# A two-layer attention and MLP kernel on Trainium2: the MLP's first product rewritten as seven smaller products

## The chip, the core and the metric

The kernel runs on one core of one Trainium2 chip. The core has five engines that run side by side, each through its own instructions in program order: TensorE (PE: matmuls, with weight loads shown apart as PEld), VectorE (DVE), ScalarE (ACT), GpSimd (POOL) and SyncE (SP), whose only work here is to issue DMA transfers. The metric is device time in microseconds (us), the median of three runs.

## The reference

Two rounds of the same pair of blocks, with the same weights, on x of 2048 rows by 640 (all float32):

```python
x = x + attention(layernorm(x), wqkv, wo)      # 32 heads of 20
x = x + mlp(layernorm(x), w1, b1, w2, b2)
# mlp: h = layernorm(x) @ w1 + b1   (640 -> 1536)
#      r = max(h, 0); h = r * r
#      out = h @ w2 + b2            (1536 -> 640)
```

## The kernel before, in words

One layer is: the projections to q, k and v; attention over 32 blocks; the output projection (`add_heads`); and the MLP in two stages, **up** (first product, with ReLU and square) and **down** (second product). The activations h go through DRAM between the two (`d_h`, `d_h1`).

Numbers are float32. For TensorE each operand is split in a high part and a rest (`split_to`: ScalarE copies, VectorE subtracts), and a product is the sum of three matmuls (`THREE`: high by high, high by rest, rest by high).

Up works on blocks of 512 rows (`qb` from 0 to 3). One of the 12 output tiles of 128 is a chain of 15 matmuls (`chain`, L376): 5 contraction tiles of 128 times the three of `THREE`, each with 128x128 weights and 512 moving columns, into one of the eight PSUM banks; the banks go round (`ps_all`). Two chains make a unit `j`; six units make a block. After a chain ScalarE applies ReLU with the bias (L1361); after a unit VectorE squares (L1369) and, for blocks whose second product is by Strassen, makes a sum and a difference (L1372, L1375).

The rows come to up normalised and transposed. For block 0 of a layer `normal_rows` normalises and TensorE turns 20 tiles (`transposed`, L1329). For blocks 1 to 3 `turned_rows` does it during the block ahead: per 128 rows, VectorE takes the statistics (L284, L285; GpSimd makes the inverse root), normalises into a tile y (L317) and transposes 32x32 squares (L322); SP writes that to DRAM (`d_t`) and reads it back turned, by four loads (`turn_load`); then `parts` splits it (L339, L340).

What an engine does beside a stage is handed out by `side()`: it takes one entry of the list `steps` at each call, so the list fixes where in each engine's own program order this side work stands. An engine that waits holds up everything behind it in its queue.

Down takes the 2048 rows in eight units of 256. Where Strassen is used, a unit has a first group of four products and a second of three (`grp` 0 and 1), each over three steps `j`; `make` prepares the operands two steps ahead, `fetch` reads h back. Weights stand split in SBUF slots of 128 x 1024 (42 slots for everything); `w_1` (120 pieces of 128, 15 slots) and `w_2` are prepared by GpSimd during the attention of layer 1 (`prep_job`), written to DRAM and loaded in every layer; 14 of the loads of `w_2` are asked for in block 0 of up, 14 in block 3.

## Time and profile before

| | |
|---|---|
| median of three runs | 3515.46 us (3514.46 to 3515.82) |
| the profiled execution: its time, its span | 3517.9 us, 3516.1 us |
| mean granted TensorE clock | 0.999 |
| busy: PE, DVE, ACT, POOL | 3504.1, 2732.5, 2733.7, 828.0 us |
| up, layer 2: its 720 matmuls | 3200.85 to 3364.08 us |
| down, layer 2 | 3364.08 us to the end |

The page gives busy time, not the use that is made of it. Matmuls are pipelined: their durations overlap, so the time a stage takes on TensorE is read from how far apart the matmuls start, not from their mean duration. In a row of the groups the last figures are the busy time in us, the mean ns of one instruction, and the idle time of the engine ahead of them with what ended it.

### The profile page before, as it was taken

The page shows a single profiled execution, that of the slowest core. Times are in us where ns is not written, and L with a number is a line of the kernel's source. Part 1 is how long each engine was busy: PE and PEld are TensorE (multiplying, and loading weights), DVE is VectorE, ACT ScalarE, POOL GpSimd, SP SyncE. Part 2 cuts the span into 40 slices and gives each one's busy share as a digit, 9 for nine tenths or more (in the row PEclk, how much of TensorE's full clock was granted, in tenths as well). Part 3 has the DMA queues.
Part 4 walks back from the last instruction along what each step waited for, and adds up shares of the span by engine and source line. Part 5 has one row for each costly group of instructions (what it writes and reads, how often), then busy time and mean ns, then how long its engine had stood idle before and what let it go on. Part 6 is the DMA issues. An engine that isn't in the chain of part 4 may idle for free.

```text
span 3516.1 us, 71077 instructions
## 1 busy us (share of the span) xinstructions
PE 3504.1 (100%) x25292; PEld 2112.9 (60%) x25292; DVE 2732.5 (78%) x5326; ACT 2733.7 (78%) x4804; POOL 828.0 (24%) x975
## 2 busy tenths in 40 slices
...
GB/s 259 234 207 188 143 170 134 135 126 133 60 55 60 42 103 192 310 198 237 234 195 224 194 180 69 77 76 57 77 76 55 53 58 50 103 196 308 195 253 141
DMA packets 325378, 514.87 MB, mean 146 GB/s; under 512 B 74532, under 2 KB 149796, under 8 KB 325024
## 3 DMA queue, kind: packets, MB, share of 16 engines
...
## 4 chain that ended last, share of the span: by engine, by line
PE 96%; DMA 2%; ACT 1%; POOL 0%; DVE 0%; issue 0%; SPq 0%; POOLq 0%; ACTq 0%; DVEq 0%
PE banks L810 28%; PE banks L795 18%; PE banks L701 18%; PE banks L376 13%; PE banks L1455 9%; PE banks L396 6%; PE banks L408 5%; PE banks L391 0%; PE banks L508 0%; ACT e L805 0%; DMA x<-d_x 0%; DMA x<-in_A_x_dram 0%; SPq L78 0%; DMA few<-d_s 0%; DMA o<-d_r 0%
## 5 line engine op out<-in xcount | busy, mean ns | idle before, releaser
L805 ACT ACTIVATE e<-banks 128x512 f32<-128x512 f32 (+1 forms) x3416 | 2035.1, 691 | 56.3 <-PE banks L795 21.5
L712 DVE TENSOR_REDUCE mx<-banks 128x1 f32<-128x512 f32 x2560 | 1620.3, 685 | 321.6 <-PE banks L701 274.4
L810 PE MATMUL banks<-e,vg 128*32 128x512 f32 x8192 | 1093.5, 605 | 2.2 <-ACT e L805 2.1
L701 PE MATMUL banks<-k,q 60*128 60x512 f32 x3360 | 1060.1, 411 | 0.9 <-DMA q<-d_qk 0.9
L795 PE MATMUL banks<-q,k 62*128 62x512 f32 x4096 | 1049.0, 441 | 1.2 <-ACT v L472 0.6
L795 PEld LDWEIGHTS banks<-q,k 62*128 62x128 f32 x4096 | 514.6, 184 | 748.5 <-ACT e L805 440.9
L701 PEld LDWEIGHTS banks<-k,q 60*128 60x128 f32 x3360 | 568.0, 185 | 196.4 <-ACT e L805 64.2
L741 DVE CUSTOM_DVE_ANT_0 rl<-banks,rl 128x512 f32<-128x512 f32 x736 | 477.0, 689 | 31.1 <-PE banks L701 6.7
L734 ACT ACTIVATE rl<-banks 128x512 f32<-128x512 f32 x736 | 399.7, 602 | 57.0 <-PE banks L701 46.5
L810 PEld LDWEIGHTS banks<-e,vg 128*32 128x32 f32 x8192 | 162.2, 108 | 353.5 <-issue 270.6
L408 PE MATMUL banks<-xnT,wqk 64*128 64x512 f32 x1080 | 327.7, 393 | 0.0
L376 PE MATMUL banks<-xnT,w 128*128 128x512 f32 x1440 | 327.0, 389 | 0.0
L396 PE MATMUL banks<-xnT,wqk 64*128 64x512 f32 x1080 | 326.9, 395 | 0.0
L376 PEld LDWEIGHTS banks<-xnT,w 128*128 128x128 f32 x1440 | 270.2, 188 | 56.0
L1361 ACT ACTIVATE r<-banks,b_t 128x512 f32<-128x512 f32 x96 | 66.2, 690 | 222.1 <-PE banks L376 205.1
L854 POOL TENSOR_TENSOR few<-few,minus_t 128x16 f32<-128x16 f32 x62 | 179.9, 2902 | 239.4 <-DMA few<-d_s 234.4
L701 PE MATMUL banks<-kd,q 60*128 60x512 f32 x736 | 210.1, 398 | 0.8 <-ACT rl L734 0.6
L408 PEld LDWEIGHTS banks<-xnT,wqk 64*128 64x128 f32 x1080 | 202.1, 188 | 8.5
L396 PEld LDWEIGHTS banks<-xnT,wqk 64*128 64x128 f32 x1080 | 200.3, 187 | 11.1 <-issue 1.7
L865 POOL TENSOR_TENSOR o<-o 128x512 f32<-128x512 f32 x62 | 79.6, 1284 | 508.6 <-DMA o<-d_r 285.5
L308 POOL CAST mr<-nt 128x32 fp32r<-128x32 f32 x64 | 13.5, 212 | 775.9 <-DVE nt L767 775.9
L396 PE MATMUL banks<-wv,xnT 64*128 64x320 f32 x960 | 193.5, 308 | 0.0
...
## 6 DMA issues: line engine op xcount, KB each, us to landing
q<-d_qk SPq DMA_DIRECT2D x876, 80.0 KB
...
k<-d_qk SPq DMA_DIRECT2D x444, 80.0 KB
...
d_o<-ot SPq DMA_DIRECT2D x248, 80.0 KB
```

What stands on the lines that cost most here:

```text
L376: nc.tensor.matmul(dst, a, b, start=(n == 0), stop=(n == last))
L396: top = nc.tensor.matmul(dst, a[:64], b[:64], start=start, stop=last)
L408: low = nc.tensor.matmul(dst, a, b, start=False, stop=last, skip_group_check=True)
L701: nc.tensor.matmul(dst, q_t[t][b : b + 60, p, sub * P : (sub + 1) * P], k_t[t // NQB, c][b : b + 60, p, :], start=True, stop=True,)
L712: nc.vector.tensor_reduce(maxima(t)[:, 2 * p + par, sub, c : c + 1], dst, axis=AX.X, op=ALU.max)
L734: nc.scalar.activation(r, dst, AF.Relu)
L741: nc.vector.tensor_tensor_reduce(out=r[par], in0=dst, in1=r[par], scale=1.0, scalar=LEAST, op0=ALU.add, op1=ALU.max, accum_out=maxima(t)[: ...
L795: nc.tensor.matmul(dst, k_t[t // NQB, kt // 4][b : b + 62, p, (kt % 4) * P : (kt % 4 + 1) * P], q_t[t][b : b + 62, p, :], start=True, stop ...
L805: nc.scalar.activation(dst, src, AF.Exp, scale=SCALE)
L810: nc.tensor.matmul(acc[32 * h : 32 * h + 32, :], v_t[t // NQB, kt // 8][:, kt % 8, 32 * h : 32 * h + 32], es[p][:, par, :], start=(kt == 0 ...
L854: nc.gpsimd.tensor_tensor(few, few, minus_t, op=ALU.pow)
L1455: nc.tensor.matmul(dst, a, b, start=first and not more, stop=last, skip_group_check=more)
```

## The change

The contraction of 640 is cut into two halves of two tiles (4 of 5 tiles) and the fifth tile. On the four tiles a unit `j`, which has 2 halves of its output (tiles j and j + 6) and 2 halves of the 512 rows, is computed by Strassen's seven products (in Winograd's form) of 128 x 256 by 256 x 256; the fifth tile is added into four of them (`extra`). A product is 6 or 9 matmuls of 256 moving columns (L1427 in the changed kernel). A unit has 54 of them, in place of 30 of 512 columns. The products stand in four banks of a half of PSUM, and three of the seven are added on top of one that VectorE has already read: S3 on S2's bank, A12 on A11's, S4 on S1's. VectorE now adds products (five additions of 256 columns a unit), ScalarE does ReLU and all squares, GpSimd makes the sum and the difference for down. S4 of a unit is issued after A11 of the next (`tail`, `finish`).

The rows of all blocks, block 0 too, are turned by VectorE and DRAM (`forms`), and for each pair of 128-row tiles GpSimd makes sums and differences, ScalarE copies the high parts and VectorE or GpSimd subtracts. `forms` has 33 or 31 yields, spread over the 42 `side()` calls of a block; for block 0 they stand in the last two blocks of `add_heads`. TensorE's transposes of up are gone.

`w_1` is prepared by `put_first` in sums and differences: 192 pieces, 24 slots; 16 are loaded in `add_heads`, 8 in block 0 of up. All 28 slots of `w_2` that down needs at first are loaded in block 3 of up (15) and in down (13), and down's first two units go side by side, so that each weight piece serves two units in a row. The matmuls of down are the same in kind and number.

TensorE, the start of up in layer 1, before (xnT: the transposed rows; w: weights) and in the changed kernel, one unit (xf, xd: the operands made by `forms`):

```order
L1329 MATMUL banks<-ident,x_16301 128x128
L376 MATMUL banks<-xnT_16461,w_15975 128x512 x3
L376 MATMUL banks<-xnT_16468,w_15975 128x512 x3
L376 MATMUL banks<-xnT_16475,w_15975 128x512 x3
L376 MATMUL banks<-xnT_16482,w_15975 128x512 x2
L376 MATMUL banks<-xnT_16482,w_15977 128x512
```

```order
L1427 MATMUL banks<-xf_16414,w_16237 128x256 x6
L1427 MATMUL banks<-xf_16420,w_16095 128x256 x6
L1427 MATMUL banks<-xf_16421,w_16095 128x256 x3
L1427 MATMUL banks<-xf_16415,w_16237 128x256 x6
L1427 MATMUL banks<-xf_16416,w_16239 128x256 x6
L1427 MATMUL banks<-xf_16417,w_16239 128x256 x6
L1427 MATMUL banks<-xd_16422,w_16243 128x256 x3
L1427 MATMUL banks<-xf_16418,w_16241 128x256 x6
```

The chain into one bank has become runs of six; the second and third row are S4 of the unit ahead.

VectorE, in the second half of block 0 of up in layer 1, before:

```order
L1369 TENSOR_TENSOR r_16757<-r_16757 128x1024
L1372 TENSOR_TENSOR s_16803<-r_16757 128x256
L1375 TENSOR_TENSOR r_16757<-r_16757 128x2x128
L340 TENSOR_TENSOR xnT_16743<-y_16653,xnT_16743 128x128
L340 TENSOR_TENSOR xnT_16745<-y_16653,xnT_16745 128x128
```

and in the changed kernel, from the tail of its second unit through its third (units counted 0 to 5: units 1 and 2; us holds u0 and u1, t is GpSimd's sums):

```order
L353 STREAM_TRANSPOSE x_16733<-y_16866 128x640
L1488 TENSOR_TENSOR r_16826<-banks,us_16749 128x2x128
L1465 TENSOR_TENSOR us_16858<-banks,us_16858 128x256
L376 TENSOR_TENSOR xf_16904<-y_16745,xf_16904 128x2x128
L376 TENSOR_TENSOR xf_16905<-t_16903,xf_16905 128x2x128
L1473 TENSOR_TENSOR us_16858<-banks,us_16858 128x256
L1474 TENSOR_TENSOR r_16941<-banks,us_16858 128x2x128
L1475 TENSOR_TENSOR r_16941<-banks,us_16858 128x2x128
```

The rests of two operands of the next block (L376: B11 and T2) now stand between the additions that read the unit's own banks (L1465 reads S2, L1473 S3, L1474 S1, L1475 A22, L1488 S4).

SP, the transfers of block 0 (d_t: the transposed tiles in DRAM; y_16773: the turned tile 2, which T2 needs), in the changed kernel:

```order
L78 DMA y_16745<-d_t 32x4x160 x4
L78 DMA d_t<-x_16731 128x640
L78 DMA d_h<-r_16723 128x1024
L78 DMA d_h_111<-us_16662 128x256
L78 DMA w_16852<-d_w_99 128x1024
L78 DMA y_16773<-d_t 32x4x160 x4
L78 DMA d_t<-x_16733 128x640
```

The load of tile 2 stands behind the write of tile 1 and two stores of unit 0.

The diff, cut to its core:

```diff
@@ -201,12 +201,16 @@
-    w_1 = Split("w1", P, NF * 2 * KD)
+    w_1 = Split("w1", P, NP * 32)
     w_2 = Split("w2", HALF, NP * 16)
-    def at_1(f, hw):
-        return ((f % NP) * 2 + f // NP) * 2 * KD + hw * KD
+    LAST = 7
+    A11, S2, S1, A22, S3, A12, S4 = range(LAST)
+    B11, T2_, T1_, T4_, T3_, B21, B22 = range(LAST)
+    def at_1(j, p, hw=0, k=0):
+        return j * 32 + p * 4 + hw * 2 + k
...
+    def put_first(j, a, b):
+        t = xtile("t")
+        k1, k2, k3 = slice(0, 2 * P), slice(2 * P, 4 * P), slice(4 * P, D)
+        def put(p, part):
+            w_1.put(part, at_1(j, p), at_1(j, p, 1), 2, pool_hi, pool_lo)
+        nc.gpsimd.tensor_tensor(t[:, k1], b[:, k1], b[:, k2], op=ALU.add)
+        pool_lo(t[:, k2], t[:, k1], a[:, k1])
+        pool_lo(b[:, k1], a[:, k1], b[:, k1])
+        put(A11, a[:, k1])
+        yield
...
-    def parts(res, i, y):
...
-    def turned_rows(qb, x_src, ys):
...
+    def forms(qb, x_src, res, late):
+        xs, ys, mvs = {}, {}, {}
+        def view(y):
+            return y.rearrange("p (a k i) -> p k a i", a=4, k=KD)
+        def split(dst, src, i, lo):
+            hi_, lo_ = (
+                dst[:, h, :, i * P : (i + 1) * P].rearrange("p k (a i) -> p k a i", a=4)
+                for h in range(2)
             )
+            nc.scalar.copy(hi_, src)
+            lo(lo_, src, hi_.bitcast(F32))
+        def pair(i):
+            a, b = view(ys[i]), view(ys.pop(i + 2))
+            t = xtile("t").rearrange("p (k a i) -> p k a i", a=4, k=KD)
+            k1, k2, k3 = slice(0, 2), slice(2, 4), slice(4, 5)
...
+            dve = nc.vector.tensor_sub
+            pool_lo(t[:, k1], b[:, k1], a[:, k1])
+            pool_lo(t[:, k2], b[:, k2], t[:, k1])
+            split(res[B11], a[:, k1], i, dve)
+            yield
+            pool_lo(b[:, k1], b[:, k2], b[:, k1])
+            split(res[T2_], t[:, k2], i, dve)
+            yield
+            split(res[T1_], t[:, k1], i, dve)
+            yield
+            pool_lo(t[:, k3], a[:, k3], b[:, k3])
+            pool_lo(t[:, k2], a[:, k2], t[:, k2])
+            split(res[B22], b[:, k2], i, dve)
+            yield
+            split(res[T4_], t[:, k2], i, pool_lo)
+            yield
+            split(res[T3_], b[:, k1], i, pool_lo)
+            yield
+            for r, y in enumerate((a, b)):
+                split(res[LAST][:, :, r : r + 1], y[:, k3], i, dve)
+            split(res[LAST + 1], t[:, k3], i, dve)
+            yield
+            if not late:
+                split(res[B21], a[:, k2], i, dve)
+                del ys[i]
+                yield
+        def rest():
+            res[B21] = slot([P, 2, 2, 2 * P], F32R, "xf")
+            for i in range(2):
+                split(res[B21], view(ys.pop(i))[:, 2:4], i, nc.vector.tensor_sub)
+        def load(i):
+            xs[i] = row_tile(x_src, qb * 4 + i)
+        def turned(i):
+            ys[i] = turn(xs[i], mvs.pop(i), i)
+            del xs[i]
+        load(0)
+        load(2)
+        yield
+        yield
+        yield
+        for i in (0, 2):
+            mvs[i] = stats(xs[i])
+            yield
+        load(1)
+        load(3)
+        yield
+        for i in (0, 2):
+            turned(i)
+            yield
+            yield
+        for i in (1, 3):
+            mvs[i] = stats(xs[i])
+            yield
+        turn_load(ys[0], 0)
+        turned(1)
+        yield
+        turn_load(ys[2], 2)
+        yield
+        turned(3)
+        yield
+        yield
+        yield
+        turn_load(ys[1], 1)
+        for n, _ in enumerate(pair(0)):
+            if n == 1:
+                turn_load(ys[3], 3)
+            yield
+        yield from pair(1)
+        if late:
+            late.append(rest)
...
-    def normal_rows(qb, x_src, res):
...
-    def transposed(xs):
...
-    def up(qb, xnt, whole, side):
...
+    class Up:
+        def __init__(self, side):
+            self.side, self.n, self.tail, self.held = side, 0, None, []
+        def chain(self, dst, j, p, x, more, extra=None):
+            todo = [
+                (w_1.piece(at_1(j, p, hw, k)), x[p][:, hx, k, :])
+                for k in range(2)
+                for hw, hx in THREE
+            ]
+            if extra is not None:
+                i, rows = extra
+                todo += [(w_1.piece(at_1(j, LAST, i) + hw), rows[:, hx, :]) for hw, hx in THREE]
+            for n, (w, v) in enumerate(todo):
+                nc.tensor.matmul(
+                    dst, w, v, start=n == 0 and not more, stop=n == len(todo) - 1,
+                    skip_group_check=more,
                 )
+        def dst(self, b):
+            return banks[:, 4 * (self.n % 2) + b, : 2 * P]
+        def finish(self):
+            if self.tail:
+                self.tail()
+                self.tail = None
+        def store(self):
+            while self.held:
+                self.held.pop(0)()
+        def flush(self):
+            self.finish()
+            self.store()
+        def unit(self, qb, j, x, whole, free):
+            side = self.side
+            us = xtile("us")
+            u0, u1 = us[:, : 2 * P], us[:, 2 * P : 4 * P]
+            last, diff = x[LAST], x[LAST + 1][:, :, 0]
+            bank = {b: self.dst(b) for b in range(4)}
+            relu = lambda out, src, f: nc.scalar.activation(
+                out, src, AF.Relu, bias=b1_t[:, f : f + 1]
+            )
+            rc = lambda z: z.rearrange("p (r c) -> p r c", r=2)
+            add = nc.vector.tensor_add
+            self.chain(bank[0], j, A11, x, False)
+            nc.scalar.copy(u0, bank[0])
+            side()
+            self.finish()
+            side()
+            self.chain(bank[1], j, S2, x, False)
+            add(u1, bank[1], u0)
+            side()
+            self.chain(bank[2], j, S1, x, False)
+            side()
+            self.chain(bank[3], j, A22, x, False, (1, diff))
+            side()
+            self.chain(bank[1], j, S3, x, True, (1, last[:, :, 1]))
+            r = slot([P, 2, 4, P], F32, "r")
+            add(u0, bank[1], u0)
+            add(r[:, 1, 1::2, :], rc(bank[2]), rc(u0))
+            add(r[:, 0, 1::2, :], rc(bank[3]), rc(u0))
+            relu(r[:, :, 1::2, :], r[:, :, 1::2, :], j + NP)
+            nc.scalar.activation(r[:, :, 1::2, :], r[:, :, 1::2, :], AF.Square)
+            side()
+            self.chain(bank[0], j, A12, x, True, (0, last[:, :, 0]))
+            relu(r[:, 0, 0::2, :], rc(bank[0]), j)
+            if free:
+                w_1.past(at_1(j, A12, 1, 1))
+            self.store()
+            side()
+            def tail():
+                self.chain(bank[2], j, S4, x, True, (0, last[:, :, 1]))
+                add(r[:, 1, 0::2, :], rc(bank[2]), rc(u1))
+                relu(r[:, 1, 0::2, :], r[:, 1, 0::2, :], j)
+                nc.scalar.activation(r[:, :, 0::2, :], r[:, :, 0::2, :], AF.Square)
+                s = u0.rearrange("p (u c) -> p u c", u=2)
                 if whole:
+                    nc.gpsimd.tensor_tensor(s, r[:, :, 2, :], r[:, :, 3, :], op=ALU.add)
+                    pool_lo(r[:, :, 2, :], r[:, :, 0, :], r[:, :, 2, :])
+                if free:
+                    w_1.past(at_1(j, LAST, 1) + 1)
+                def store():
+                    dma(nc.sync, d_h[qb, j].rearrange("p u c -> p (u c)"),
+                        r.rearrange("p u q c -> p (u q c)"))
                     if whole:
+                        dma(nc.sync, d_h1[qb, j].rearrange("p u c -> p (u c)"), u0)
+                self.held.append(store)
+            self.tail = tail
+            self.n += 1
...
             self.steps = [
+                (un, grp, j) for grp in (0, 1) for j in range(NP // 2) for un in range(2)
+            ]
+            self.steps += [
                 (un, grp, j)
-                for un in range(2 * NQB)
+                for un in range(2, 2 * NQB)
                 for grp in ((0, 1) if un < 2 * blocks else (2,))
                 for j in range(NP // 2)
             ]
...
+                while self.uses and self.uses[0][0] <= n + (
+                    3 if n < NP or self.uses[0][1] == 2 * NQB - 1 and self.blocks < NQB else 5
+                ):
                     self.fetch()
...
+        coming = first_forms = None
         for qb in range(NQB):
-            if qb + 1 == NQB:
-                rows = []
-                norm = normal_rows(0, x_m, rows)
-                steps.extend([lambda: (next(norm, None), next(norm, None))] * 5)
+            if qb == 2:
+                first_forms = forms(0, x_m, x := {}, [])
+            if qb > 1:
+                steps.extend([lambda: [next(first_forms, None) for _ in range(3)]] * 7)
             add_heads(qb, x_a, x_m, xs, side)
-            for s in range(qb * 4, min(qb * 4 + 4, w_1.n)):
+            for s in range(qb * 4, qb * 4 + 4):
                 w_1.load(s)
             if qb > 1:
                 all_steps()
+        for _ in first_forms:
+            pass
         w_o.drop()
-        xnt = transposed(rows)
         blocks = NQB if ahead is None else NQB - 1
         down = Down(blocks, x_m, x_e)
-        coming = [s for s in range(w_2.n) if s not in slots_of(W12)]
+        coming = [0, 1, 4, 5, 6, 7, 2, 8, 9, 10, 11, 3, 12, 13, 14, 15]
+        coming += [16, 17, 18, 24, 25, 19, 20, 21, 26, 22, 23, 27]
         def bring(n):
             for _ in range(n):
                 if coming:
                     w_2.load(coming.pop(0))
-        norm = turned_rows(1, x_m, ys := [])
-        next(norm)
+        firsts = list(range(16, w_1.n))
+        up = Up(side)
         for qb in range(NQB):
+            nxt, late = {}, []
             if qb + 1 < NQB:
+                late.append(None)
+                coming_rows = forms(qb + 1, x_m, nxt, late)
+                for n in range(7 * NP - 1):
+                    steps.append(lambda n=n, f=coming_rows: (
+                        n % 2 == 1 and firsts and w_1.load(firsts.pop(0)), next(f, None)
+                    ))
             else:
+                todo = {35: down.fetch, 37: lambda: down.rows(0), 36: down.fetch, 38: down.make,
+                        39: down.fetch, 41: down.make}
+                for n in range(7 * NP):
+                    steps.append(lambda n=n: (
+                        n in todo and todo[n](), bring(int(n % 7 in (1, 4) or n % 14 == 6))
+                    ))
+            for j in range(NP):
+                up.unit(qb, j, x, qb < blocks, qb == NQB - 1)
             all_steps()
+            if late:
+                for _ in coming_rows:
+                    pass
+                del x[B21]
+                late[1]()
+            x = nxt
+        up.flush()
         w_1.drop()
+        down.rows(1)
```

158 lines of the change are left out of this document (39 added, 119 removed).

## The prediction

> **What bounds the kernel now.** I read the page's busy shares and its chain first, then the chain in order of time for the MLP of layer 2, then groups, windows and timelines of up.
>
> ```profile
> PE 3504.1 (100%) x25292; PEld 2112.9 (60%) x25292; DVE 2732.5 (78%) x5326; ACT 2733.7 (78%) x4804; POOL 828.0 (24%) x975
> PE 96%; DMA 2%; ACT 1%; POOL 0%; DVE 0%; issue 0%; SPq 0%; POOLq 0%; ACTq 0%; DVEq 0%
> ```
>
> TensorE is busy throughout and is 96% of the chain that ended last. What saves TensorE time in up shows in full; so does every wait that TensorE is given.
>
> ```profile
> 3128.82 50.61 PE banks L376 x345
> ...
> 3196.67 1.13 DVE x L292 x2
> 3198.77 2.08 PE banks L1329 x17
> 3200.85 163.23 PE banks L376 x720
> 3364.08 146.44 PE banks L1455 x996
> ```
>
> Up of layer 2 is 720 matmuls of 512 columns in 163.23 us, 226.7 ns each, without a gap; the output projection ahead of it is 345 of 320 columns in 50.61 us, 146.7 ns each. The difference is 80.0 ns for 192 columns, 0.417 ns a column, with 13.2 ns to spare for each matmul.
>
> ```profile
> L376 PE MATMUL banks<-xnT,w 128*128 128x512 f32 x1440 | 327.0, 389 | 0.0
> L1329 PE MATMUL banks<-ident,x 128*128 128x128 f32 x20 | 2.3, 273 | 0.0
> L1369 DVE TENSOR_TENSOR r<-r 128x1024 f32<-128x1024 f32 x23 | 28.0, 1217 | 53.2 <-ACT r L1361 53.2
> ```
>
> The second row is layer 1's transposes alone: 20 in 2.3 us, 115 ns each, so a new 128x128 weight load every 115 ns can be had. The third is why up has no gap: VectorE waits for ScalarE, ScalarE for TensorE, and nobody makes TensorE wait, since a finished chain is read one bank of eight later.
>
> **The matmuls.** 1440 of 512 columns (326.5 us) go; 54 x 24 x 2 = 2592 of 256 columns come. The trace has none of 256. Bounds: not under the 115 ns of a bare weight load (298 us), not over the 146.7 ns of 320 columns (380 us). The line through the two rows gives 120.0 ns, just over the weight load; I take it, 311.0 us: **15.5 us less**.
>
> The Trainium skill, "TensorE: Matmul & The Clock Gate", section "Back-to-back issue gap", gives columns / 2.4 + 2.5 ns, as an estimate 109 ns at 256 columns: 283 us, 28 us better than my sum. Its 2.5 ns are 13.2 ns in this trace, so I stay with the rows.
>
> **The transposes.** Layer 1 loses 2.3 us; in layer 2 the stretch from 3196.67 to 3200.85, 4.2 us, in which TensorE waits for VectorE between transposes. **6.5 us less.** Block 0's `forms` run beside `add_heads`, where VectorE has room:
>
> ```profile
> 1400.00:1420.00 20.00, 20.00 (x138) 20.00 (x138) 4.43 (x9) 0.00 (x0) 0.00 (x0) 1.00 0.78 284
> 1447.00:1487.00 40.00, 40.00 (x178) 33.10 (x177) 26.23 (x46) 12.27 (x33) 9.89 (x20) 1.00 1.00 356
> 3326.00:3366.00 40.00, 40.00 (x182) 33.30 (x182) 13.35 (x20) 9.81 (x15) 0.00 (x0) 1.00 0.87 307
> ```
>
> Columns: PE, PEld, DVE, ACT, POOL busy, clock, DMA share, GB/s. 4.43 of 20 us for VectorE there; its own additions may fall behind by eight banks, 8 x 15 x 0.147 = 17.6 us, before TensorE notices. I cost block 0 at nothing; without that cover it is one turning round, some 10 us a layer.
>
> **What TensorE now waits for.** This is the term that decides. S4 is added on S1's bank, so it may start only when L1474 has read that bank, and L1474 needs L1473, which needs S3. From the end of S3 to the start of S4 TensorE has A12 (9 matmuls) and A11 of the next unit (6): 15 x 0.12 = 1.8 us. VectorE needs 0.2 us to see S3 (a 320-column matmul lasts 309 ns and is followed after 147) and two additions of 0.42, some 1.1 us. **0.7 us of slack** stands against whatever side work is ahead of L1473 in VectorE's queue. Durations:
>
> ```profile
> L1434 DVE TENSOR_TENSOR s<-s,r 128x256 f32<-128x256 f32 x42 | 17.6, 419 | 0.0
> L1455 PE MATMUL banks<-w,hb 128*128 128x320 f32 x504 | 83.2, 309 | 0.0
> L317 DVE TENSOR_SCALAR y<-x,mv 128x640 f32<-128x640 f32 x24 | 21.9, 913 | 0.0
> L322 DVE STREAM_TRANSPOSE x<-y 128x640 f32<-128x640 f32 x24 | 20.3, 846 | 0.8
> L284 DVE BATCH_NORM_STATS2 bst<-x 128x6 f32<-128x320 f32 x128 | 54.9, 471 | 40.4 <-DMA x<-d_x 37.9 <-DMA x<-in_A_x_dram 2.5
> L285 DVE BATCH_NORM_AGGREGATE mv<-bst 128x2 f32<-128x12 f32 x64 | 13.4, 209 | 2.2
> L311 POOL TENSOR_TENSOR w<-raw,w 128x256 fp32r<-128x256 f32 x6 | 4.4, 737 | 0.0
> L296 ACT CAST hd<-s 128x256 fp32r<-128x256 f32 x42 | 17.1, 407 | 54.3 <-DVE s L1442 54.3
> L1361 ACT ACTIVATE r<-banks,b_t 128x512 f32<-128x512 f32 x96 | 66.2, 690 | 222.1 <-PE banks L376 205.1
> ```
>
> and for a load of a turned tile, SP's issues and the reader of their first four (of eight), in layers 1 and 2:
>
> ```profile
> 1476.86 0.38 SPq L78 DMA_DIRECT2D d_h<-r  x1
> 1477.28 0.43 SPq L78 DMA_DIRECT2D d_h<-s  x1
> 1477.81 4.15 SPq L78 DMA_DIRECT2D y<-d_t  x8
> ```
> ```profile
> 1481.99 1.10 ACT L339 CAST xnT<-y 128x128 fp32r<-128x128 f32 x5 [0.59 <-DMA y<-d_t]
> ```
> ```profile
> 3232.62 4.52 SPq L78 DMA_DIRECT2D y<-d_t  x8
> ```
> ```profile
> 3238.08 1.10 ACT L339 CAST xnT<-y 128x128 fp32r<-128x128 f32 x5 [2.48 <-DMA y<-d_t]
> ```
>
> From the first issue to the reader it is 4.2 and 5.5 us. Even before, the readers waited for these loads; it cost TensorE nothing.
>
> First wait, in the third unit. Its L1473 stands behind T2's rest. Counted from the end of S3 of the second unit: 0.2, three additions 1.26, then tile 1 is normalised and turned (0.91 + 0.85): 3.2 us. SP writes it and issues unit 0's two stores (0.34 + 0.38 + 0.43), and only then loads tile 2: 4.4; its reader has it at 8.6. GpSimd makes t in two steps (1.47), ScalarE copies (0.41), VectorE subtracts (0.42): 10.9. L1473 and L1474 add 0.84: 11.7 us. TensorE, unhindered, asks for S4 of the third unit after 69 matmuls, 8.3 us. **3.4 us late.**
>
> Second wait, a unit on. T2 of the second pair needs GpSimd's sums, and these stand behind the sum and difference of the unit ahead, which need its S4. From the end of that S4: 0.2, addition 0.42, ReLU 0.5 (between the copy and L1361), square 0.69, five GpSimd operations 3.7, copy 0.41, rest 0.42, two additions 0.84: 7.2 us, against 45 matmuls or 5.4 us: 1.8 us late; 3.6 where L1488 itself stands behind the rests of T1 and B22, which wait for ScalarE's ReLU and square of the unit ahead.
>
> Smaller ones: the turnings (0.91 + 0.85) and statistics (2 x 0.47 + 0.21) that fall ahead of L1465, which S3 waits for: some 0.5 us a block.
>
> That is 5.7 to 7.5 us in a block, and blocks 0, 1, 2 of both layers have it. The bounds: if tile 2 came 1 us sooner and the queues met as well as they can, 4.1; with block 0's weight loads ahead of tile 2 (DMA share 1.00 above) and every wait full, 8.5. I take 7.5, the upper of the two sums, since the orders leave no way round these waits: 6 x 7.5 = **45 us more** (25 to 51).
>
> **The rest at nothing.** The first 16 slots of `w_1` come under `add_heads` (DMA 0.78), the last 8 in block 0, due at its fifth unit 26 us in; 8 x 512 KB at 356 GB/s take 12. `w_2`: 15 slots in block 3 where there were 14 (0.87), 13 in down, the first of them due after six steps of 24 x 0.147 = 21 us. GpSimd's extra preparation lies under the attention of layer 1, where it is 0% of the chain. If one of these covers fails it is 2 to 3 us a layer. VectorE per block: 30 additions and 16 rests of 0.42 at most (19.3), four statistics (4.6), four turnings (7.0): 31 of 39 us, so it is late, not full.
>
> **Sum** against the profiled execution: 3517.9 - 15.5 - 6.5 + 45 = 3540.9 us. That execution lies 2.4 us over the median of the runs: **3538.5 us**, 0.7% slower. By itself 3518 to 3546.
>
> **Rivals.** (1) The waits are hidden: tile 2 lands early enough, or GpSimd and ScalarE finish sooner than their rows say. For it: VectorE has 8 us to spare in a block, and 0.7 us of slack meets most additions. It decides from the point where GpSimd has tile 2 at 5.2 us in place of 8.6, and the second chain is 2 us shorter too. Against it: the 3.2 us before tile 1 can be written and the 4.2 us of the load alone make 7.4. It gives 3515.5 - 22 = 3493.5, faster by 0.6%. (2) Half of it: waits of 2 to 4 us a block, 12 to 24 in all, cancel the 22: 3505 to 3518. (3) TensorE's clock falls as well.
>
> ```profile
> 1788.37 0.79 PE L701 MATMUL banks<-k,q 60*128 60x512 f32 x1 [0.86 <-DMA q<-d_qk]
> 1788.00:1791.00 3.00, 2.63 (x12) 2.16 (x14) 1.45 (x3) 0.00 (x0) 0.00 (x0) 0.55 0.56 211
> 3095.00:3127.00 32.00, 30.73 (x206) 9.47 (x207) 1.38 (x2) 29.45 (x33) 6.08 (x4) 1.00 0.56 181
> ```
>
> After a wait of 0.86 us the granted clock was 0.55 for 3 us, which loses some 1.4. Twelve waits of 2 us and more, each with that: up to 17 us, 3556; with some of the other terms at their upper ends 3570. Against it: where TensorE idled 1.3 of 32 us (the last row) the clock stayed at 1.00, and the lost clock is partly lost while TensorE would wait anyway.
>
> The Trainium skill, same page, Part 1, has the clock halve after an idle window of about 3.4 us; by that rule these waits would seldom do it and rival (3) adds nothing. The row above shows it after less.
>
> (4) 256 columns cost more than the line says, up to 146.7 ns: 69 us more than I take.
>
> **Chances.** Forecast 0.63; clock or matmul price on top (3, 4) 0.11; hidden (1) 0.18; half (2) 0.08, most of it within 0.2%. A difference under 0.2% (7 us) cannot be told from none here: faster 0.20, same 0.06, slower 0.74. The range reaches up into (3) and down to the upper part of (1): 3495 to 3567.
>
> **What would show it.** Matmuls of L1427 starting 120 ns apart where they run undisturbed. Idle time of TensorE ahead of L1427 put down to L1474 (and L1465), two waits of 2 to 4 us in the third and fourth unit of blocks 0 to 2 and none in block 3, so up of some 178 us in a layer: four blocks of 38.9 and three times 7.5. VectorE's T2 row waiting for ScalarE, that for GpSimd, that for the loads of y. Wrong would be: up under 165 us in a layer (rival 1), a clock under 1 in up (3), or waits that begin at a weight load.

## The result: 2.8% slower, and the profile after

The changed kernel takes 3612.70 us (median of 4 runs, 3611.53 to 3612.81) against 3515.35 us before: a ratio of 1.0276, 95% interval 1.0259 to 1.0294. Forecast were 3538.5 us, 3495 to 3567. The direction is right, the size is 74 us short.

Its profiled execution took 3612.81 us (span 3610.7, mean clock 0.988; before 3517.9, 3516.1 and 0.999). The page's busy shares, and the group of the new matmuls:

```profile
PE 3519.4 (97%) x26404; PEld 2177.0 (60%) x26404; DVE 2771.0 (77%) x5512; ACT 2834.9 (79%) x5026; POOL 965.2 (27%) x1189
L1427 PE MATMUL banks<-xf,w 128*128 128x256 f32 x2448 | 331.6, 297 | 74.4 <-DVE r L1474 64.9
```

TensorE was at 100% and is at 97%. The row of the old matmuls (L376) had 0.0 us of idle time in front; this one has 74.4, and 64.9 of it ends with VectorE's L1474, the addition that the prediction named.

The blocks of up in layer 1, one window each (columns as in the prediction's windows):

```profile
1444.00:1512.00 68.00, 45.90 (x327) 44.37 (x326) 33.81 (x76) 24.36 (x59) 24.93 (x39) 0.82 0.69 238
1512.00:1561.40 49.40, 42.95 (x327) 41.74 (x326) 29.36 (x66) 24.28 (x57) 22.03 (x34) 0.93 0.47 159
1561.40:1611.10 49.70, 42.85 (x326) 42.04 (x326) 29.26 (x66) 24.37 (x56) 22.02 (x34) 0.93 0.47 162
1611.10:1651.00 39.90, 39.07 (x326) 38.87 (x325) 14.75 (x36) 20.62 (x41) 1.48 (x2) 1.00 0.87 298
```

Undisturbed a block is 324 x 0.120 = 38.9 us. Block 3, which prepares no rows, nearly has that; blocks 1 and 2 lose 10.5 and 10.8, and block 0 loses 29. The clock (seventh figure) is 0.82 and 0.93 where they lose. The blocks of layer 2 take 67.9, 49.7, 49.9 and 43.0 us.

For the budget I took the distance from the start of each matmul of up to the start of the next. What exceeds 120 ns is counted as waiting where the distance is over 250 ns, and as lost clock where it is 200 to 250 ns (at half clock the matmuls start 213 ns apart).

| both layers, us | forecast | measured |
|---|---|---|
| matmuls of 256 columns (up's 326.2 to 311) | -15.5 | -15.2 |
| transposes and the step into up | -6.5 | -5.9 |
| waits in blocks 1 and 2 | +30 | +30.8 (7.6, 7.5; 8.1, 7.6) |
| waits in block 0 | +15 | +47.0 (23.9; 23.1) |
| waits in block 3 | 0 | +4.5 (1.0; 3.5) |
| half clock in up | 0 | +23.4 |
| down, longer (159.5 to 164.8; 148.0 to 153.2) | 0 | +10.5 |
| sum | +23.0 | +95.1 |

The profiled executions differ by 94.9.

**Blocks 1 and 2 go as forecast.** VectorE, ScalarE, GpSimd and SP's issues around the first wait of block 1, then TensorE:

```profile
1530.65 0.77 DVE L376 TENSOR_TENSOR xf<-y,xf 128x256 fp32r<-128x256 f32 x1 [1.21 <-ACT xf L375]
1534.98 0.49 DVE L376 TENSOR_TENSOR xf<-t,xf 128x256 fp32r<-128x256 f32 x1 [3.57 <-ACT xf L375]
1535.40 0.41 DVE L1473 TENSOR_TENSOR us<-banks,us 128x256 f32<-128x256 f32 x1
1535.85 0.42 DVE L1474 TENSOR_TENSOR r<-banks,us 128x256 f32<-128x256 f32 x1
...
1545.65 0.50 DVE L376 TENSOR_TENSOR xf<-t,xf 128x256 fp32r<-128x256 f32 x1 [1.89 <-ACT xf L375]
```
```profile
1534.55 0.41 ACT L375 CAST xf<-t 128x256 fp32r<-128x256 f32 x1 [3.93 <-POOL t L342]
```
```profile
1531.21 0.80 POOL L342 TENSOR_TENSOR r<-r 128x256 f32<-128x256 f32 x1
1532.98 0.72 POOL L342 TENSOR_TENSOR t<-y,y 128x256 f32<-128x256 f32 x1 [0.97 <-DMA y<-d_t]
1533.79 0.73 POOL L342 TENSOR_TENSOR t<-y,t 128x256 f32<-128x256 f32 x1
```
```profile
1528.53 2.55 SPq L78 DMA_DIRECT2D y<-d_t  x4
```
```profile
1536.32 6.03 PE L1427 MATMUL banks<-xf,w 128*128 128x256 f32 x27 [3.70 <-DVE r L1474]
```

Read from the bottom: TensorE waits 3.70 us (forecast 3.4) for L1474; that and L1473 stand behind T2's rest (1534.98), the rest waits for ScalarE's copy, the copy for GpSimd's second sum, the first sum for tile 2, which arrives 4.5 us after its first issue. The rest at 1545.65 is the second pair's: it costs TensorE 1.6 us, and 0.6 more a unit on, against 1.8 forecast (in block 2 it is 2.6 at once).

**Block 0 does not.** SP's issues, then the readers, then TensorE:

```profile
1442.90 8.69 SPq L78 DMA_DIRECT2D d_x<-x  x4
1451.68 1.88 SPq L78 DMA_DIRECT2D w<-d_w  x4
1453.67 0.95 SPq L78 DMA_DIRECT2D x<-d_x  x2
```
```profile
1460.37 0.89 DVE L315 BATCH_NORM_STATS2 bst<-x 128x6 f32<-128x320 f32 x2 [8.79 <-DMA x<-d_x]
...
1485.08 0.49 DVE L376 TENSOR_TENSOR xf<-t,xf 128x256 fp32r<-128x256 f32 x1 [6.62 <-ACT xf L375]
```
```profile
1463.29 5.12 PE L1427 MATMUL banks<-xf,w 128*128 128x256 f32 x27 [8.52 <-DVE r L1474]
...
1486.42 3.78 PE L1427 MATMUL banks<-xf,w 128*128 128x256 f32 x16 [7.99 <-DVE r L1474]
```

Block 0's 23.9 us are 4.2 at its start (2.9 in layer 2), where `forms` of block 0 is late, three waits of 8.7, 8.1 and 2.1, and 0.7 in short stops. The 8.7 are a wait that the prediction did not have: in the first unit VectorE's statistics stand ahead of L1473, on row tiles that are issued at 1453.67, behind four loads of `w_1`, and land at 1460.4. SP is that late because it stands 8.69 us at the last stores of `add_heads`, whose additions are late behind `forms` of block 0. The 8.1 are the forecast first wait, which was to be 3.4, and the 2.1 the forecast second one. Layer 2 has the same: 8.9, 8.5 and 2.1.

**Down** waits at its start for operands that `make` has not made:

```profile
1659.65 1.68 DVE L1593 TENSOR_TENSOR x<-x,b_t 128x640 f32<-128x640 f32 x2 [2.37 <-DMA x<-d_x]
1663.46 0.43 DVE L1561 TENSOR_TENSOR s<-s,r 128x256 f32<-128x256 f32 x1 [2.14 <-DMA s<-d_h]
```

VectorE waits for the second unit's rows, then for a fetched tile; TensorE stops for 2.2 us and runs 3.4 us at half clock.

### The profile page after: what moved, and what is told of

The parts are those of the page before. It is cut to its first block, busy times and chain, and to the rows that moved or that the text cites. A ratio compares the mean times of both kernels' runs of the same rounds, so it can differ in the third digit from the quotient of the medians.

```text
span 3610.7 us, 74267 instructions
## 1 busy us (share of the span) xinstructions
PE 3519.4 (97%) x26404; PEld 2177.0 (60%) x26404; DVE 2771.0 (77%) x5512; ACT 2834.9 (79%) x5026; POOL 965.2 (27%) x1189
## 5 line engine op out<-in xcount | busy, mean ns | idle before, releaser
L1427 PE MATMUL banks<-xf,w 128*128 128x256 f32 x2448 | 331.6, 297 | 74.4 <-DVE r L1474 64.9
L1427 PEld LDWEIGHTS banks<-xf,w 128*128 128x128 f32 x2448 | 320.7, 205 | 81.9 <-DVE r L1474 68.6
L954 POOL TENSOR_TENSOR few<-few,minus_t 128x16 f32<-128x16 f32 x62 | 179.9, 2902 | 236.1 <-DMA few<-d_s 236.0
L339 POOL CAST mr<-nt 128x32 fp32r<-128x32 f32 x64 | 13.6, 212 | 751.1 <-DVE nt L867 751.1
L496 PEld LDWEIGHTS banks<-xnT,wqk 64*128 64x128 f32 x1080 | 199.2, 186 | 11.5 <-issue 1.7
L1454 ACT ACTIVATE r<-r,b_t 128x512 f32<-128x512 f32 x96 | 59.2, 616 | 170.9 <-DVE r L1475 149.2
```

The source lines that it names most:

```text
L496: top = nc.tensor.matmul(dst, a[:64], b[:64], start=start, stop=last)
L954: nc.gpsimd.tensor_tensor(few, few, minus_t, op=ALU.pow)
L1427: nc.tensor.matmul(dst, w, v, start=n == 0 and not more, stop=n == len(todo) - 1, skip_group_check=more,)
```

## The experiments

Each is an edit of the changed kernel. Idle figures are TensorE's, by the reckoning above. Times are single runs, but for the changed kernel, e14 and e17 (medians of four), e10 and e11 (two) and e15 (seven); the kernel before took 3515 to 3516 us beside them. The four runs of e17 lie between 3542.3 and 3553.1 us, so a difference of a few us between single runs shows nothing by itself; the waits are read from the traces.

| run | us | up, layers 1; 2 | block 0 idle | blocks 1, 2 idle (layer 1) |
|---|---|---|---|---|
| changed kernel | 3612.7 | 206.9; 210.4 | 23.9; 23.1 | 7.6, 7.5 |
| e1 no forms | 3516.4 | 159.3; 162.5 | 2.4; 3.1 | 0, 0 |
| e2 splits on GpSimd | 3601.2 | 203.0; 204.4 | 23.2; 21.7 | 7.9, 7.2 |
| e3 pair late | 3594.6 | 200.6; 199.7 | 19.2; 18.5 | 6.6, 6.9 |
| e4 `w_1` late | 3609.2 | 205.4; 206.7 | 19.8; 21.6 | 7.8, 7.5 |
| e5 sums early | 3596.2 | 197.3; 202.7 | 18.5; 18.2 | 6.4, 6.5 |
| e6 rows later | 3599.0 | 201.0; 204.2 | 19.0; 17.7 | 8.4, 7.3 |
| e7 fetch early | 3600.5 | 203.7; 206.2 | 21.7; 22.2 | 8.9, 7.5 |
| e8 = e5, e6 (five calls), e7 | 3575.8 | 190.2; 193.3 | 13.6; 14.4 | 6.9, 6.5 |
| e9 = e5, rests later | 3578.5 | 188.9; 192.9 | 17.6; 17.1 | 4.9, 4.8 |
| e10 all | 3550.2 | 180.9; 182.0 | 11.5; 12.3 | 3.5, 4.4 |
| e11 all, first forms earlier | 3549.8 | 179.9; 181.0 | 12.5; 12.5 | 3.9, 4.4 |
| e13 rows ahead | 3604.6 | 202.3; 207.1 | 17.8; 19.2 | 7.7, 7.5 |
| e14 all, rows ahead | 3547.7 | 179.8; 181.0 | 11.8; 10.2 | 4.0, 4.4 |
| e15 no forms, fetch early | 3505.2 | 160.0; 161.6 | 2.9; 3.5 | 0, 0 |
| e16 `w_1` apart | 3603.1 | 197.1; 202.9 | 15.1; 15.5 | 7.8, 7.8 |
| e17 all, `w_1` apart | 3548.4 | 179.7; 181.0 | 9.4; 9.7 | 3.3, 4.6 |

### e1: is it all the side work?

```diff
-                coming_rows = forms(qb + 1, x_m, nxt, late)
+                coming_rows = iter(())
...
-                del x[B21]
-                late[1]()
-            x = nxt
```

> Blocks 1 to 3 use the operands of block 0 again: their rows are not loaded, normalised, turned or split (that part of the computation is left out); the loads of w_1, the order of matmuls and the additions of up stay. If all that up lost lies in waits on the forms work and in the clock that falls behind them, up becomes four blocks of 38.9 us, 155 to 159 us in a layer in place of 206.9 and 210.4, at a clock of 1.00, and the run about 3507 us (3612.8 less 51 and 54, at most 8 us off). If the matmuls of 256 columns, or the additions between the chains, cost something by themselves, up stays over 165 us in a layer and the run over 3520 us.

Measured: 159.3 and 162.5 us of up, 3516.4 us. Its blocks 0 and 1 in layer 1:

```profile
1443.90:1485.50 41.60, 39.68 (x326) 39.05 (x325) 17.18 (x42) 18.48 (x40) 10.08 (x14) 1.00 0.74 285
1485.50:1524.40 38.90, 38.90 (x326) 38.90 (x325) 12.18 (x30) 18.62 (x37) 8.83 (x12) 1.00 0.26 103
```

Block 1 is 38.90 us with TensorE busy for 38.90, at full clock: the matmuls of 256 columns and the additions between the chains cost nothing more. So up's loss is the side work and its clock, but for some 4 and 7 us that blocks 0 and 3 keep (2.4 and 3.1 us of waiting at the start, where `forms` of block 0 is late, and 1.0 and 3.1 at the end, where operands of down are late). The run is 9 us over the forecast sum, a little more than the 8 allowed: down keeps its 4.7 and 6.1 us. Without the side work of blocks 1 to 3 the change brings nothing as long as down keeps its loss (e15 takes that away too): no repair of this side work alone can do better.

### e2: the splits of T1 and T2 on GpSimd

```diff
-            split(res[T2_], t[:, k2], i, dve)
+            split(res[T2_], t[:, k2], i, pool_lo, pool_hi)
...
-            split(res[T1_], t[:, k1], i, dve)
+            split(res[T1_], t[:, k1], i, pool_lo, pool_hi)
```

> The splits of T1 and T2 (rounded copy and rest) go from ScalarE and VectorE to GpSimd, as late as before. Theory A (place in the queue: VectorE's rest of T2 and ScalarE's copy stand ahead of what S4 needs): the waits in the third and fourth unit go, some 7 us in blocks 1 and 2 and the 8.1 us in block 0; block 0's first wait of 8.7 us, for the row tiles, stays; up about 170 to 180 us in a layer, the run 3535 to 3560 us. Rival (the data are late for whoever reads them next, or GpSimd becomes the queue): B22's copy waits in T2's place, up stays over 195 us in a layer, the run over 3590 us.

The rival held. T2 no longer stands in VectorE's queue, but the next operand that needs GpSimd does: ScalarE's copy for T4 waits 4.44 us for a GpSimd that now has four operations more ahead of it, and VectorE's next rest waits for ScalarE. Blocks 1 and 2 keep 7.9 and 7.2 us.

### e3: the pair seven calls later

```diff
         turn_load(ys[0], 0)
+        turn_load(ys[2], 2)
         turned(1)
         yield
-        turn_load(ys[2], 2)
         yield
...
+        for _ in range(7 if late else 0):
+            yield
         turn_load(ys[1], 1)
```

> The load of turned tile 2 is issued ahead of tile 1's turning, and the first pair's sums and splits begin seven side calls (6.5 to 7 us) later; nothing else moves. Theory A: T2's rest meets a tile that is there, so the waits of blocks 1 and 2 fall from some 7 to at most 2 us each and block 0's second wait from 8.1 to at most 3; block 0's first, 8.7 us for the row tiles, stays; with the clock that comes back up is about 180 to 187 us in a layer, the run 3560 to 3575 us. Rival (GpSimd's chain behind the sums of the unit ahead sets the wait, whenever the pair begins): the waits move seven calls later and keep their size, up stays over 200 us in a layer, the run over 3600 us.

Tile 2 is there, and the first wait falls from 3.9 to 1.46 us; but the second grows from 1.6 to 3.84. GpSimd's sums stand behind the sum and difference of the unit ahead, whenever the pair begins. That is the prediction's second chain, and its upper figure (3.6 us) was nearer than its sum (1.8). Blocks 1 and 2 win only 0.6 to 1 us of 7.5: the waits moved and nearly kept their size, as the rival had it, though the run (3594.6 us) falls between the two forecasts.

### e4: the loads of `w_1` later

```diff
-                        n % 2 == 1 and firsts and w_1.load(firsts.pop(0)), next(f, None)
+                        n > 12 and n % 2 == 1 and firsts and w_1.load(firsts.pop(0)), next(f, None)
```

> The last eight slots of w_1 are loaded from the fourteenth side call of block 0 on, in place of the second; nothing else moves. Theory B (the loads of w_1 stand ahead of the row tiles and the turned tiles in SP's queue and in DRAM): block 0's waits fall from 23 us to the 7 us of the other blocks, 16 to 20 us less in a layer with the clock, the run 3573 to 3582 us. Theory A2 (the row tiles are late because SP stands 8.7 us at add_heads' last stores, and the pair's order makes the rest): the first wait falls only to 4 to 5 us, the second to 5, 7 to 8 us less in a layer, the run about 3597 us.

The run is only 3.5 us shorter, less than either theory gave. The first wait is 7.5 us: the four loads at 1451.5, which come under `add_heads`, still stand ahead of the row tiles. The second falls from 8.1 to 5.7 (in layer 2 from 8.5 to 6.3).

### e5: GpSimd's sums ahead of their readers

```diff
+            pool_lo(b[:, k1], b[:, k2], b[:, k1])
+            pool_lo(t[:, k3], a[:, k3], b[:, k3])
+            yield
             split(res[B11], a[:, k1], i, dve)
             yield
-            pool_lo(b[:, k1], b[:, k2], b[:, k1])
             split(res[T2_], t[:, k2], i, dve)
+            pool_lo(t[:, k2], a[:, k2], t[:, k2])
...
+        first, second = pair(0), pair(1)
+        next(first)
+        yield
+        turn_load(ys[3], 3)
+        for _ in range(3 if late else 0):
+            yield
+        for n, _ in enumerate(first):
+            if n == 3:
+                next(second)
...
```

The load of turned tile 2 moves ahead of tile 1's turning as in e3, and the splits of T4 and T3 change places (not shown).

> GpSimd's sums of each pair are issued three or four side calls ahead of the copies and rests that read them (T4's two calls), and the load of turned tile 2 ahead of tile 1's turning; the row loads, the loads of w_1 and down stay as they are. Theory A2 (what ScalarE's copy and VectorE's rest wait for is GpSimd, which takes its sums after the unit's sum and difference): the waits of 3.7 to 3.9 and 1.5 to 2.6 us of blocks 1 and 2 go, the two of 0.6 us for the turnings stay; block 0's 8.1 and 2.1 fall to at most 3 in all, its first of 8.7 stays; with the clock up is 175 to 182 us in a layer, the run 3548 to 3560 us. Rival (the queues of VectorE and ScalarE are simply full, so work that moves takes its wait along): up stays over 195 us in a layer, the run over 3585 us.

Theory A2 fell at blocks 1 and 2. GpSimd is in time, and 6.4 us are still lost, now all of it to L1472, the addition of S2 that S3 waits for (L1465 of the changed kernel): 0.67, 0.59, 1.84 and 3.32 us in block 1, and nearly the same in block 2. VectorE and ScalarE at the last of them:

```profile
1542.54 0.42 DVE L1495 TENSOR_TENSOR r<-banks,us 128x256 f32<-128x256 f32 x1
1544.56 0.68 DVE L376 TENSOR_TENSOR xf<-t,xf 128x256 fp32r<-128x256 f32 x1 [1.60 <-ACT xf L375]
1545.16 0.41 DVE L1472 TENSOR_TENSOR us<-banks,us 128x256 f32<-128x256 f32 x1
```
```profile
1542.99 0.51 ACT L1461 ACTIVATE r<-r,b_t 128x256 f32<-128x256 f32 x1 [0.83 <-DVE r L1495]
1543.53 0.63 ACT L1497 ACTIVATE r<-r 128x512 f32<-128x512 f32 x1
1544.07 0.69 ACT L375 CAST xf<-t 128x256 fp32r<-128x256 f32 x2
```

The copy stands behind ReLU and square of the unit ahead, these behind VectorE's L1495, and VectorE's rest, issued in the same call as its copy, stands idle for 1.60 us ahead of L1472. GpSimd had made the sum by 1538.5; by these rows it is the order in ScalarE's queue, which e9 tries.

### e6: block 0's statistics nine calls later

```diff
+        for _ in range(9 if qb == 1 else 0):
+            yield
         for i in (0, 2):
             mvs[i] = stats(xs[i])
```

> In block 0 alone the statistics of the coming rows, and with them all that follows, stand nine side calls (some 9 us) later; the row tiles are loaded where they were. Theory A2 (VectorE takes statistics, ahead of L1473, on row tiles that have not landed): the first wait of block 0 falls from 8.7 us to under 1; its second, 8.1 us, falls to some 4 to 5, the size of blocks 1 and 2, if it was the loads of w_1 that made y's load slow there, and stays if not; the run is 3576 to 3592 us. Rival (what is not waited for there is waited for later): up within 4 us of 206.9 and 210.4, the run over 3604 us.

```profile
1472.94 0.89 DVE L315 BATCH_NORM_STATS2 bst<-x 128x6 f32<-128x320 f32 x2 [6.31 <-DMA x<-d_x]
```

The first wait is nearly gone (0.6 us) and another of 7.1 us came some 14 us later: the second pair of row tiles, issued at 1462.7 behind seven more loads of `w_1`, lands only at 1472.9. Block 0's idle time falls by 5 us, not by 8 or more, and the run (3599.0 us) lies between the two forecasts.

### e7: down's fetches early

```diff
-                todo = {35: down.fetch, 37: lambda: down.rows(0), 36: down.fetch, 38: down.make,
-                        39: down.fetch, 41: down.make}
+                todo = {30: down.fetch, 31: down.fetch, 34: down.fetch, 36: down.fetch,
+                        37: lambda: down.rows(0), 38: down.make, 41: down.make}
...
-                    3 if n < NP or
+                    4 if n < NP or
```

> In block 3 down's first fetches are issued five side calls earlier, the fourth there too, and the next ones a step earlier; up to that place nothing changes. If down's longer start (2.3 us of waiting and 3.4 us of half clock in layer 1, 3.3 us of waiting in layer 2) comes from fetches that land late behind the loads of w_2, down is 160 and 149 us in place of 164.8 and 153.2, the wait of 1.0 and 3.2 us at the end of up goes too, and the run is 3600 to 3604 us. If it comes from the two-unit order itself (more operands to be made by VectorE and ScalarE at the start), down stays as it was and the run over 3609 us.

The run is 3600.5 us, as forecast. Down of layer 1 is 160.5 us (from 164.8), block 3 is 39.0 and 39.5 us (from 40.0 and 43.0): late fetches it was. Down of layer 2 stays at 152.9, against 149 forecast: there VectorE waits for the second unit's rows, which are loaded behind up's last stores. With these early too (e10) it is 149.2.

### e8: the three together

The edits of e5, e6 (five calls) and e7.

> The sums ahead, the statistics of block 0 five calls later, and the early fetches together. If the three causes are separate, up is 162 to 168 us in a layer, down 160 and 149, and the run 3512 to 3525 us, at a clock of 0.997 or more; if one of them only moves a wait to the next queue, over 3540 us.

They nearly add up (e5 -16, e6 with its nine calls -14, e7 -12 us; together -37), so the causes are largely separate, but the forecast of 3512 to 3525 us had taken each to go as a whole. 27 and 28 us of waiting stay in a layer, with e5's 1.84 and 3.3 us in blocks 1 and 2.

### e9: each rest one call behind its copy

```diff
             nc.scalar.copy(hi_, src)
-            lo(lo_, src, hi_.bitcast(F32))
+            pend.append(lambda: lo(lo_, src, hi_.bitcast(F32)))
```

on top of e5; what is pending is issued at the start of the next call, and GpSimd's last sum of a pair moves one call later too.

> As the kernel with the sums ahead, and each rest (VectorE's or GpSimd's) stands one side call behind its rounded copy, in place of the same call. Theory A3 (with GpSimd's sums there in time, the wait is VectorE's rest for a copy that stands in ScalarE's queue behind the ReLU and square of the unit ahead, 1.84 and 3.3 us ahead of L1465's addition in each of blocks 1 and 2): these two go, the 0.6 us of the turnings stay; block 0 loses its 2.3 and 4.1 too and keeps 8 us; with the clock up is 176 to 186 us in a layer in place of 197.3 and 202.7, the run 3552 to 3565 us. Rival (VectorE and ScalarE are full, so that the order inside their queues changes nothing): within 6 us of the 3596 us of the sums alone.

The waits of 1.84 and 3.32 us become stops of 0.3, 1.4, 0.95 and 0.4; the two of 0.6 to 0.7 stay, and one of 0.6 comes at the block's start. Blocks 1 and 2 lose 4.9 us in place of 6.4, and hardly any clock (0.7 us in place of 1.8). The gain is 18 us, half of what theory A3 gave; block 0 keeps its 17.

### e10 and e11: all repairs

e10 has e9, e6 (five calls), e7, the transposes of the turned tiles one call behind their normalising, and the second unit's rows in block 3:

```diff
             ys[i] = turn(xs[i], mvs.pop(i), i)
-            del xs[i]
+            pend.append(lambda: turn_rest(xs.pop(i), ys[i], i))
...
+                        39: lambda: down.rows(1)}
...
-        down.rows(1)
```

e11 also starts block 0's `forms` one block of `add_heads` earlier:

```diff
-            if qb == 2:
+            if qb == 1:
                 first_forms = forms(0, x_m, x := {}, [])
-            if qb > 1:
-                steps.extend([lambda: [next(first_forms, None) for _ in range(3)]] * 7)
+            if qb:
+                steps.extend([lambda: [next(first_forms, None) for _ in range(2)]] * 7)
```

> The sums ahead, the rests one call later, the transposes of the turned tiles one call behind their normalising, the statistics of block 0 five calls later, down's fetches and the rows of its second unit early. Theory A3: no wait over 1 us is left in blocks 1 and 2; block 0 keeps its first 4 to 5 us for forms that come late; up 160 to 167 us in a layer, down 160 and 149 to 150, the run 3508 to 3524 us, clock 0.997 or more. Rival (full queues): over 3550 us.

> As the run with everything, and the forms of block 0 begin a block of add_heads earlier, two steps a call in place of three. If up's first 4 to 5 us come from VectorE's being late there, they go: 4 to 5 us a layer less, the run 3500 to 3515 us. If the early forms push add_heads' own additions or find no free buffer, the output projection becomes longer than 71.2 us and the run is no faster than the one before.

3550.2 us, 1.0099 times the time before (1.0070 to 1.0129), and 3549.8 (1.0098; 1.0069 to 1.0127): two thirds of the loss are mended, and both forecasts were 26 to 50 us too low; the rival of full queues had over 3550 us for e10, which is where it came out. Blocks 1 and 2 still lose some 4 us, in stops of 1.5 us and less. In e11 the start of up is free of waits, but the output projection takes 72.5 us in place of 71.2 and the row tiles bring back a wait of 8.5, so it is no faster than e10, as its rival had it.

### e12: planted waits

```diff
+            for _ in range(planted):
+                nc.vector.transpose(self.scratch[1], self.scratch[0])
             add(u0, bank[1], u0)
```

> As the kernel without forms (the rows of blocks 1 to 3 are left out), with 1 to 12 transposes of a scratch tile (0.85 us each) planted in VectorE's queue ahead of L1473's addition: 1 and 2 in the third and sixth unit of block 1 of layer 1, 3 and 4, 5 and 6 in blocks 2 and 3, and 7 to 12 in layer 2. The slack of S4 by the prediction's sum (0.7 us) makes TensorE wait 0.85 k less some 0.75 us: 0.1, 0.9, 1.8, ... 9.4 us. Theory C (the clock halves after any wait of a microsecond or so, for longer after a longer one): half clock behind every plant from the second on, 3.4 us behind the short and 6.8 to 10.2 behind the long. Rival (it takes a wait of 3.4 us and more): none behind the plants of 1 to 4.

This is e1's kernel with 1 to 12 transposes of a scratch tile ahead of L1473. TensorE behind 7, 8 and 9 of them:

```profile
3268.43 4.99 PE L1427 MATMUL banks<-xf,w 128*128 128x256 f32 x27 [2.70 <-DVE r L1476]
...
3293.19 4.81 PE L1427 MATMUL banks<-xf,w 128*128 128x256 f32 x27 [3.57 <-DVE r L1476]
...
3318.65 5.61 PE L1427 MATMUL banks<-xf,w 128*128 128x256 f32 x27 [4.46 <-DVE r L1476]
```

Each transpose more costs 0.88 us, but the first four cost next to nothing: 7 x 0.88 - 2.70 = 3.5 us of room, not 0.75. Work that is ready runs while TensorE does S1, A22 and S3 (24 x 0.12 = 2.9 us) and takes up that time too; the prediction's 0.7 us holds only for work that becomes ready after S3 (2.9 + 0.7 is close to the 3.5). So up to 3.5 us of work costs nothing here if it is ready, and work that comes late costs at once.

The clock in windows of 3.4 us (PE busy is the second figure, the clock the seventh):

```profile
3265.50:3268.90 3.40, 0.70 (x6) 0.50 (x6) 3.10 (x6) 0.16 (x1) 0.00 (x0) 1.00 0.18 69
3268.90:3272.30 3.40, 3.40 (x19) 3.40 (x18) 0.85 (x2) 2.95 (x6) 0.20 (x1) 0.50 0.03 7
3272.30:3275.70 3.40, 3.40 (x30) 3.40 (x30) 0.77 (x2) 0.00 (x0) 1.28 (x2) 1.00 0.36 147
...
3313.30:3316.70 3.40, 0.90 (x8) 0.69 (x6) 3.26 (x5) 0.00 (x0) 0.00 (x0) 1.00 0.38 147
3316.70:3320.10 3.40, 1.45 (x6) 1.45 (x7) 2.16 (x5) 1.10 (x2) 0.00 (x0) 0.50 0.00 0
3320.10:3323.50 3.40, 3.40 (x17) 3.40 (x17) 0.85 (x2) 2.02 (x5) 0.73 (x1) 0.50 0.00 0
3323.50:3326.90 3.40, 3.40 (x31) 3.40 (x30) 1.12 (x3) 0.00 (x0) 0.73 (x1) 1.00 0.50 193
```

Half clock comes one window behind a window in which TensorE did little, and full clock one window behind a busy one. A busy window at half clock holds 19 matmuls in place of 28: it costs 1.1 us or more. After the stop of 5 transposes (0.94 us) the clock stayed at 1.00. Neither theory had it right: what counts is the window, not the length of one wait.

### e13 to e17: what holds block 0

```diff
+            if qb == 3:
+                nxt, late = {}, [None]
+                coming_rows = forms(1, x_m, nxt, late)
+                next(coming_rows)
             add_heads(qb, x_a, x_m, xs, side)
```

> The row tiles 0 and 2 of block 1 are loaded ahead of the last block of add_heads, so ahead of its four stores, on which SP stands 8.7 us, and of the last loads of w_1 that follow them; nothing else moves. Theory B2 (block 0's first wait is the row tiles' 7 us in the DMA queues behind those loads): the first wait falls from 8.7 to under 1.5 us, the second and third stay, 9 to 12 us less in a layer with the clock, the run 3588 to 3596 us. Rival (as with the statistics nine calls later: the wait goes over to the second pair of row tiles, which still stands behind the loads of w_1): a wait of 5 us or more for x at the second pair's statistics, less than 5 us a layer, the run over 3602 us.

```profile
1450.39 0.89 DVE L315 BATCH_NORM_STATS2 bst<-x 128x6 f32<-128x320 f32 x2 [0.26 <-DMA x<-d_x]
...
1464.18 0.89 DVE L315 BATCH_NORM_STATS2 bst<-x 128x6 f32<-128x320 f32 x2 [6.23 <-DMA x<-d_x]
```

Rows 0 and 2 are there in time and the wait goes over to rows 1 and 3, as the rival had it: issued at 1454.5 behind six loads of `w_1`, landed at 1464.2. e16 therefore takes `w_1` out of the way of both:

```diff
             for s in range(qb * 4, qb * 4 + 4):
-                w_1.load(s)
+                if qb < 3:
+                    w_1.load(s)
...
-        firsts = list(range(16, w_1.n))
+        firsts = list(range(12, w_1.n))
...
-                        n % 2 == 1 and firsts and w_1.load(firsts.pop(0)), next(f, None)
+                        (5 < n < 12 or 19 < n < 26) and firsts and w_1.load(firsts.pop(0)), next(f, None)
```

> Row tiles 0 and 2 of block 1 ahead of add_heads' last block as before, and the last twelve slots of w_1 (four of which followed add_heads' stores) loaded at side calls 6 to 11 and 20 to 25 of block 0: behind the second pair of row tiles, and not while the turned tiles come back. Theory B3 (block 0's waits above 7.5 us are row tiles and turned tiles that stand in the DMA queues behind w_1): the two waits for x go (7.9 and 2.5 us with row tiles 0 and 2 alone ahead), T2's wait is 3.5 to 4.5 us as in blocks 1 and 2 in place of 8.1, block 0 loses 7 to 9 us in all in place of 23; up 184 to 190 us in a layer, the run 3565 to 3578 us. Rival (it is VectorE's own lateness behind add_heads that block 0 pays): block 0 keeps over 14 us, the run over 3592 us.

VectorE's first statistics, and its longer waits after them:

```profile
1450.18 0.89 DVE L315 BATCH_NORM_STATS2 bst<-x 128x6 f32<-128x320 f32 x2 [0.20 <-DMA x<-d_x]
...
1460.95 0.94 DVE L348 TENSOR_SCALAR y<-x,mv 128x640 f32<-128x640 f32 x1 [1.30 <-POOL mv L319]
...
1474.09 1.09 DVE L376 TENSOR_TENSOR xf<-t,xf 128x256 fp32r<-128x256 f32 x2 [2.75 <-ACT xf L375]
```

No wait for x is left (the second pair of row tiles, issued at 1452.1 with no load of `w_1` in the 8 us ahead of it, is read without a wait at 1457.6), and T2's is 4.35 us (4.7 in layer 2), about what theory B3 said; block 0 has 8.8 and 7.6 us less than in the changed kernel. But 15 us stay where 7 to 9 were expected, and the run is 3603.1: by these two figures the rival holds. Up itself is 9.8 and 7.5 us shorter, and the run only 9.6: some 8 us are lost again outside up, and no run shows why. What stays in block 0 is in the main 2.2 us at the start, 2.9 us for the second pair's statistics and turnings, which now come in one lump, T2, and 2.9 us for the second pair's rests.

e14 and e17 are e11 without the five extra calls ahead of the statistics and with the loads of the diffs above: e14 with e13's and e4's, e17 with e13's and e16's. e15 is e1 with e7's fetches and e10's early rows.

> Everything of the last combined kernel, with row tiles 0 and 2 of block 1 loaded ahead of add_heads' last block, the last eight slots of w_1 from the fourteenth call on, and no extra calls ahead of the statistics in block 0. If block 0's waits are the DMA queue behind the loads of w_1, block 0 comes to the 4 to 5 us that blocks 1 and 2 lose now: up 169 to 174 us in a layer, the run 3528 to 3540 us. If the row tiles are still late, as in the combined kernel: within 5 us of 3549.8 us.

> The last combined kernel with the same places for the loads of w_1. By theory B3 its waits of 5.5, 2.9 and 2.8 us in block 0 go to some 4 us in all, as in blocks 1 and 2: 7 to 9 us a layer with the clock, up 170 to 174 us, the run 3528 to 3536 us, 0.4 to 0.6% slower than before: the additions still have no room for all the side work. Rival: within 4 us of 3547.7 us.

> The kernel without forms (the rows of blocks 1 to 3 are left out) with down's fetches and rows early: what the change could give if its side work cost nothing. By the sum: 3516.4 less the 2.9 us and 3.4 us that down waits at its start and half a window of clock in each layer, 3505 to 3510 us, faster than before by 0.15 to 0.3%. If down's two-unit order costs something by itself, 3513 us or more, no faster than before.

e14 gives 3547.7 us (1.0093; 1.0078 to 1.0108), e17 3548.4 (1.0089; 1.0072 to 1.0105): both as their rivals had it. Block 0 gains up to 3 us of waiting and gives it back (in e17 TensorE waits 3.1 us in the output projection and 3.5 us for a slot of `w_1`). e15 gives 3505.2 us, as forecast, 0.9972 times the time before (0.9960 to 0.9983): down is 159.5 us in layer 1, as before, and 150.2 in layer 2 (148.0), so most of what its two-unit order cost was late fetches. That 0.28% is all that the change gave with the side work of blocks 1 to 3 left out. No run with the side work in it beats the kernel before.

## Why the prediction was right in direction and wrong in size

**Matmuls, right.** 1052 and 1035 of the 1296 in a layer are followed after exactly 120 ns; the line through the two rows held. The 283 us that the prediction worked out from the Trainium skill, "TensorE: Matmul & The Clock Gate", section "Back-to-back issue gap", were not seen; the section gives that formula for the gap of matmuls by themselves, without their weight loads.

**Transposes, right** to 0.6 us. "I cost block 0 at nothing", in the same paragraph, is where the first error begins. The additions of `add_heads` did fall behind `forms`, and TensorE noticed for some 4 us of layer 1. But SP noticed too: it stood 8.69 us at the stores, and everything behind them came later.

**Waits, right in place and mechanism, mis-sized in block 0.** "6 x 7.5" holds for four of its six blocks (7.5 to 8.1), for the reason given: e1 takes the side work away and they go, e3 and e5 move them from one named link to the next. In block 0 the term measured 23.9 and 23.1 us in place of 7.5. The step that failed is the one on `w_1`: "The first 16 slots of `w_1` come under `add_heads`, the last 8 in block 0". Four of the 16 were issued when up had begun, ahead of the row tiles; I priced their bandwidth and the time at which they are due, not who stands behind them. For the statistics I added durations and never asked when their rows land. Behind `w_1` the row tiles land 6.7 us after their issue (changed kernel), 10.2 (e6) and 9.7 (e13); with the first pair issued ahead of the stores and no `w_1` just ahead of the second they are waited for no more (e16), and that takes away about 8 of the 16 us too many. How much of it is SP's stand at the stores and how much `w_1` is not told apart. The late `forms` at the start are 2.9 to 4.2, and y's loads behind `w_1` some more (e4's second wait, 5.7 in place of 8.1). For the rest no run gives one cause: e17, with every repair, still has 9.4 us in block 0.

**Clock: put at nothing in the sum, a rival that came on top.** Rival (3) had up to 17 us and 11 in 100 together with (4); it is 23.4, of which 12.1 fall in blocks 1 and 2, whose waits were as forecast. I set against it a row where TensorE idled 1.3 of 32 us at full clock; e12 shows why this proves little: single windows of 3.4 us count, and 1.3 us of idle time leave each of them busy for 2.1 or more. The sentence from the Trainium skill, "TensorE: Matmul & The Clock Gate", Part 1, by which rival (3) would add nothing, was not borne out.

**"The rest at nothing" failed for down**: 10.5 us, and 4.5 us in block 3, all from fetches and rows that land late (e7, e10, e15). The cover that I named, 21 us before a slot of `w_2` is due, was that of the weights; `make`'s own inputs were not looked at.

Of the 74 us by which the forecast fell short, block 0 has 32, the clock 23, down and block 3 15. Either of the first two put right alone would leave the time above 3567; both together would bring it to 3557. The chance of 0.74 for slower stands; the range's upper end allowed for the clock of rival (3), but not for block 0. (A slip in the sum: 25 to 51 us more than 3493.5 is 3518 to 3545, not 3546; nothing rests on it.)
